# First four chunks with the masks ahead of the conversions and no zero products between; row tiles 2 to 5 converted whole

## The chip, the cores and the metric

One core of one Trainium2 chip. The time is device microseconds (us) of one launch. The engines are named as in the profile: PE (TensorE), DVE (VectorE), ACT (ScalarE), POOL (GpSimd) and SP (SyncE, which issues transfers).

## The reference

Three layers follow each other, all in float32; the two sets of MoE weights arrive as 64-bit floats.

```
state = gamma * state + k_t v_t^T;  y_t = scale * q_t state          # (4, 8, 768, 64) retention
x = y as (3072, 512)
h = x @ w_in (512 -> 2048);  g = h if h > 0 else exp(h) - 1;  x2 = g @ w_out (2048 -> 512)
out = max(x2 @ w1, x2 @ w2, x2 @ w3) (512 -> 768 each) @ moe2_w_out (768 -> 512)
```

## The kernel before

The 3072 tokens are six blocks of 512, each block four chunks of 128. A product of two float32 operands is made of three passes: each operand is split into a high part (float32r, written by ACT) and a low part (the rest, written by DVE), and high x high, high x low and low x high are added up in one accumulator.

The first MoE layer works through 16 row tiles f of `wa`; each holds 128 x 512 columns of `w_in` (used by `h1`, which makes 512 hidden values of a block) and 128 x 512 of `w_out` (used by `o1`, which adds to four accumulators). A weight arrives as two 32-bit words. Turning 512 columns (a half, number n; row tile f has the halves 2f and 2f + 1) into a high and a low part takes six operations: `cv_bits` (ACT scales the upper word), `cv_rest` (three DVE operations: shift, sign, lower word), `cv_high` (ACT) and `cv_low` (DVE).

The span begins with the retention of the first four chunks, which need no earlier state: `wide_scores` (PE), `wide_mask` (DVE), `wide_mix` (PE, then the high part on ACT), `wide_rest` (the low part on DVE). Between them stand `junk` products of a zeroed tile on PE. Behind them `h1` of block 0 starts. From chunk 4 on a `visit(c)` does the retention of one chunk: `values` (PE; two guard copies on ACT at L240), `open_chunk` of the next one (scores and state update on PE, mask on DVE at L182), `finish` (PE `past` at L219, high part on ACT at L251, low part on DVE at L254) and `ready` (POOL L207, L155 and L145; DVE L210 and L212). In the program, visits 4 to 6 alternate with row tiles 2 to 4 of block 0 (`lead`), then block 1 begins (`h1(1, 0)`).

In this part the order on PE, DVE, ACT, POOL and SP is the order in which the code is written: every engine takes its own list in turn, and an instruction that waits holds all behind it. `h1` ends in exp (L398), relu (L399), e (DVE L402), gh (ACT L405) and gl (DVE L410). In what follows e(0,f) is the L402 of row tile f in block 0.

Of the kernel before, what the change touches and what calls it, by code (L numbers as in the profile page):

```python
# [17 lines left out]
P = 128  # L18
# [24 lines left out]
def kernel(ctx: ExitStack, tc: tile.TileContext, qkv0, qkv, wa, wb, dmask, qdec, cols, out):  # L43
# [26 lines left out]
    def f32(ap):  # L70
        return ap.bitcast(F32)
# [187 lines left out]
    def wide_scores(c):  # L259
        qk = raw_t[c][0]  # L260
        sc = sc_t[c] = [ps_acc.tile([P, NPAIR, P], F32, tag="acc", name="sc") for _ in range(2)]
        for p, g, r, n in heads():
            nc.tensor.matmul(
                sc[g][:, n, :], qk[rows(g), p // 2, 2 + r, :], qk[rows(g), p // 2, r, :],
                start=n == 0, stop=n == NPAIR - 1,
            )

    def wide_mask(c):
        if not wide:
            wide[0] = wpool.tile([P, 2, 2, NPAIR, P], F32, tag="w", name="a")  # L270
        sc, a = sc_t.pop(c), wide[0][:, c % 2]
        for g in range(2):
            nc.vector.tensor_tensor(
                out=a[:, g].rearrange("t (i r) q -> t i r q", r=2), in0=sc[g].rearrange("t (i r) q -> t i r q", r=2),
                in1=dmask_of(g), op=ALU.mult,
            )
        a_t[c] = a
# [23 lines left out]
            nc.tensor.matmul(up[rows(g), n, :], kd[:, p, r, :], v[:, p, r, :], start=n == 0, stop=n == NPAIR - 1)  # L301
        nc.scalar.copy(home[c], up)

    w_t, half = {}, []

    sources = [wa[n // 2][:, n % 2 * 512:(n % 2 + 1) * 512] for n in range(2 * KFF)]

    raws = {}
    DEEP = 10

    def load_half(n):
        if n < len(sources):
            f = n // 2
            if f % 2 and f < DEEP:
                if n % 2 == 0:
                    raws[f] = wpool.tile([P, 2, 512, 2], I32, tag="w", name="raw")
                r = raws[f][:, n % 2]
            else:
                r = stage.tile([P, 512, 2], I32, tag="raw", name="raw")
            nc.sync.dma_start(out=r.rearrange("p n w -> p (n w)"), in_=sources[n].bitcast(I32))  # L320
            half.append(r)

    def load_halves(n):
        while len(half) < min(n, len(sources)):
            load_half(len(half))

    tmp, keys = {}, [("a", f) for f in range(KFF)]

    def cv_bits(n):
        if n // 2 >= len(keys):  # L330
            return
        t = tmp[n] = dpool.tile([P, 512], I32, tag="t", name="t")
        nc.scalar.activation(f32(t), f32(half[n][:, :, 1]), ACTF.Copy, scale=2.0 ** -112)

    def cv_rest(n):
        if n // 2 >= len(keys):
            return
        t = tmp[n]
        lo, hi = half[n][:, :, 0], half[n][:, :, 1]
        nc.vector.tensor_scalar(  # L340
            out=t, in0=t, scalar1=3, scalar2=0x7FFFFFFF, op0=ALU.logical_shift_left, op1=ALU.bitwise_and
        )
        nc.vector.scalar_tensor_tensor(  # L343
            out=t, in0=hi, scalar=-0x80000000, in1=t, op0=ALU.bitwise_and, op1=ALU.bitwise_or
        )
        nc.vector.scalar_tensor_tensor(
            out=t.bitcast(U32), in0=lo.bitcast(U32), scalar=29, in1=t.bitcast(U32),
            op0=ALU.logical_shift_right, op1=ALU.bitwise_or,
        )
        load_halves(n + 1 + (4 if n + 4 < 2 * DEEP else 2))  # L350

    def cv_high(n):
        key, c = keys[n // 2], n % 2
        if c == 0:
            w_t[key] = wpool.tile([P, 2, 2 * 512], F32R, tag="w", name="w")
        nc.scalar.copy(w_t[key][:, 0, c * 512:(c + 1) * 512], f32(tmp[n]))  # L356

    def cv_low(n):
        key, c = keys[n // 2], n % 2
        w = w_t[key][:, :, c * 512:(c + 1) * 512]  # L360
        nc.vector.tensor_tensor(out=w[:, 1], in0=f32(tmp.pop(n)), in1=f32(w[:, 0]), op=ALU.subtract)  # L361

    PASSES = ((1, 0), (0, 1), (0, 0))

    FRESH = ((0, 0), (0, 1), (1, 0))
# [17 lines left out]
    def h1(b, f, then=(), after=(), mid=(), soon=(), next_=()):  # L383
        x = x_t[b]
        w = w_t["a", f]
        hp = ps_h.tile([P, BLK], F32, tag="h", name="hp")
        order = [(kk, pw, px) for kk in range(KDM) for pw, px in PASSES]
        if fresh(b, f):
            order = [(kk, pw, px) for pw, px in FRESH for kk in range(KDM)]
        for k, (kk, pw, px) in enumerate(order):  # L390
            nc.tensor.matmul(  # L391
                hp, w[:, pw, kk * P:(kk + 1) * P], x[px][:, kk, :],
                start=k == 0, stop=k == len(order) - 1,
            )
        e = gpool.tile([P, BLK], F32, tag="e", name="e", bufs=3)
        gh = gpool.tile([P, BLK], F32R, tag="gh", name="gh")
        gl = gpool.tile([P, BLK], F32R, tag="gl", name="gl")
        nc.scalar.activation(e, hp, ACTF.Exp)  # L398
        nc.scalar.activation(e, e, ACTF.Relu, scale=-1.0, bias=1.0)  # L399
        for step, n in mid:  # L400
            step(n)
        nc.vector.scalar_tensor_tensor(out=e, in0=e, scalar=-1.0, in1=hp, op0=ALU.mult, op1=ALU.max)  # L402
        for step, n in soon:
            step(n)
        nc.scalar.copy(gh, e)  # L405
        for step, n in next_:
# [414 lines left out]

    FA, FB = 5, 9
    groups = [(0, 0, FA), (1, 0, FB), (0, FA, KFF), (1, FB, KFF)]
    groups += [(b, 0, KFF) for b in range(2, NB)]
    seq = [(b, f, f0, f1) for b, f0, f1 in groups for f in range(f0, f1)]
# [38 lines left out]
    def junk(k):  # L866
        o = ps_h.tile([P, BLK], F32, tag="h", name="junk")
        for i in range(k):
            nc.tensor.matmul(o, zero[:, 0:P], zero, start=i == 0, stop=i == k - 1)
# [29 lines left out]
    def lead(f):
        n = 2 * f + 1  # L900
        cv_rest(n)
        cv_high(n)
        cv_rest(n + 1)
        cv_low(n)
        h1(0, f, (), (), (), [(cv_high, n + 1)], [(cv_low, n + 1)])

    def bits(f):
        cv_bits(2 * f + 1)
        cv_bits(2 * f + 2)
# [10 lines left out]
    wide_scores(2)  # L920
    wide_mask(2)
    cv_bits(0)
    wide_mix(1)
    cv_rest(0)
    cv_high(0)
    wide_rest(1)
    wide_scores(3)
    wide_mask(3)
    wide_mix(2)
# [258 lines left out]
```

## Time and profile before

| what | us |
|---|---|
| median of 3 runs (lowest, highest) | 974.17 (973.41, 974.77) |
| the profiled execution, its span | 975.89, 974.1 |
| PE busy | 955.2 (98% of the span) |
| DVE, ACT, POOL busy | 567.8, 347.8, 104.5 |
| chain that ended last, by engine | PE 86%, DVE 6%, issue 3%, ACT 2%, DMA 2% |

Busy time counts an instruction from start to end. A wait is read as the idle time of an engine just before an instruction, with the engine and line that ended it.

### The profile page before, as it was taken

How to read it: one execution, taken by the hardware profiler on the slowest of the kernel's cores; microseconds unless marked ns; L12 is line 12 of the kernel's file. 1: busy time of each engine (PE TensorE's matmuls, PEld its weight loads, DVE VectorE, ACT ScalarE, POOL GpSimd, SP SyncE). 2: the span in 40 equal slices, each digit the busy share in tenths (PEclk: the TensorE clock that was granted, in tenths of full speed). 3: DMA queues.
4: the chain of work that ended last, by engine and by line, in shares of the span. 5: the costliest groups of instructions: out<-in, count | busy, mean ns of one | idle time of the engine just before them, and what ended most of it. 6: DMA issues, size and time to landing. Idle time of an engine off the chain costs nothing.

```text
span 974.1 us, 16007 instructions
## 1 busy us (share of the span) xinstructions
PE 955.2 (98%) x6642; PEld 778.9 (80%) x6643; DVE 567.8 (58%) x931; ACT 347.8 (36%) x630; POOL 104.5 (11%) x136
## 2 busy tenths in 40 slices
PE   7899999999999999999999999999999999999998
PEld 4677878887888888878887888878888788888886
DVE  4886777434556565655554652577734777336650
ACT  2545565333444544454445453121210213101111
POOL 3230010123111111111100000000000000000100
PEclk9999999999999999999999999999999999999999
DMA  9843164236345555545535452556525565246602
GB/s 313 247 166 121 53 208 138 31 101 174 101 146 164 164 163 172 164 164 163 163 130 180 157 188 71 173 173 198 180 97 206 176 208 167 98 130 205 200 5 87
DMA packets 65928, 149.68 MB, mean 154 GB/s; under 512 B 5120, under 2 KB 35584, under 8 KB 59712
## 3 DMA queue, kind: packets, MB, share of 16 engines
q1 hardware_dynamic: 53472, 86.78, 27.7%
q0 software_dynamic: 8784, 55.06, 18.0%
q10 hardware_dynamic: 3600, 6.82, 1.9%
q8 instruction: 52, 0.85, 0.4%
q14 instruction: 20, 0.16, 0.1%
HBM read 114.30 MB, written 34.34 MB: 153 GB/s over the span
## 4 chain that ended last, share of the span: by engine, by line
PE 86%; DVE 6%; issue 3%; ACT 2%; DMA 2%; SPq 1%; POOL 0%; ACTq 0%; POOLq 0%; DVEq 0%
PE hp L744 25%; PE acc L429 24%; PE hp L391 23%; PE acc L804 10%; DMA x<-in_qkv 2%; PE xs L230 1%; DVE t L343 1%; PE xs L219 1%; DVE e L402 1%; PE xs L168 1%; ACT gh L405 1%; PE xs L196 1%; DVE t L340 1%; DMA x<-x2d 1%; DVE w L361 1%
## 5 line engine op out<-in xcount | busy, mean ns | idle before, releaser
L744 PE MATMUL hp<-seat,w 128*128 128x512 f32 x1134 | 259.9, 390 | 3.4 <-DVE m L753 3.4
L744 PEld LDWEIGHTS hp<-seat,w 128*128 128x128 f32 x1134 | 212.1, 188 | 49.9 <-DVE m L753 6.1
L391 PE MATMUL hp<-xh,w 128*128 128x512 f32 x768 | 246.1, 392 | 1.5 <-ACT w L356 0.8
L429 PE MATMUL acc<-gh,w 128*128 128x512 f32 x768 | 203.7, 394 | 1.6 <-ACT gh L405 0.5
L391 PEld LDWEIGHTS hp<-xh,w 128*128 128x128 f32 x768 | 144.8, 189 | 32.5 <-ACT xh L289 1.1
L429 PEld LDWEIGHTS acc<-gh,w 128*128 128x128 f32 x768 | 141.6, 188 | 34.6 <-ACT gh L405 1.7
L402 DVE SCALAR_TENSOR_TENSOR e<-e,hp 128x512 f32<-128x512 f32 x96 | 65.8, 685 | 135.0 <-ACT e L399 134.6
L391 PE MATMUL hp<-xl,w 128*128 128x512 f32 x384 | 142.6, 392 | 0.0
L429 PE MATMUL acc<-gl,w 128*128 128x512 f32 x384 | 109.6, 390 | 0.0
L398 ACT ACTIVATE e<-hp 128x512 f32<-128x512 f32 x96 | 57.1, 594 | 119.2 <-PE hp L391 113.2
L804 PE MATMUL acc<-w,g 128*128 128x512 f32 x432 | 99.1, 389 | 0.0
L410 DVE TENSOR_TENSOR gl<-e,gh 128x512 fp32r<-128x512 f32 x96 | 67.3, 701 | 49.9 <-ACT gh L405 48.2
L804 PEld LDWEIGHTS acc<-w,g 128*128 128x128 f32 x432 | 81.1, 188 | 16.8
L405 ACT CAST gh<-e 128x512 fp32r<-128x512 f32 x96 | 59.7, 621 | 88.8 <-DVE e L402 88.8
L391 PEld LDWEIGHTS hp<-xl,w 128*128 128x128 f32 x384 | 72.7, 189 | 15.6 <-DVE xl L254 0.3
L429 PEld LDWEIGHTS acc<-gl,w 128*128 128x128 f32 x384 | 72.1, 188 | 15.2
L770 ACT COPY u<-hp 128x512 f32<-128x512 f32 x27 | 15.9, 589 | 143.4 <-PE hp L744 142.4
L638 POOL DMA_DIRECT2D w<-ops_d x48 | 25.6, 533 | 381.9 <-PE hp L744 311.5
L399 ACT ACTIVATE e<-e 128x512 f32<-128x512 f32 x96 | 60.8, 633 | 3.1
L145 POOL TENSOR_TENSOR x<-x,cols_sb 128x512 f32<-128x512 f32 x24 | 27.1, 1133 | 158.8 <-DMA x<-in_qkv 158.8
L761 ACT CAST g<-e 128x512 fp32r<-128x512 f32 x36 | 22.2, 623 | 51.9 <-DVE e L758 51.5
L753 DVE TENSOR_TENSOR t<-hp,t 128x512 f32<-128x512 f32 x45 | 31.0, 689 | 12.3 <-PE hp L744 12.3
(92 smaller groups left out, 810.3 us busy)
## 6 DMA issues: line engine op xcount, KB each, us to landing
w<-ops_d POOLq DMA_DIRECT2D x48, 1024.0 KB, 5.2
x<-in_qkv SPq DMA_DIRECT2D x44, 512.0 KB, 6.1
ops_d<-m SPq DMA_DIRECT2D x66, 256.0 KB, 3.2
raw<-in_wa SPq DMA_DIRECT2D x32, 512.0 KB, 4.7
raw<-in_wb SPq DMA_DIRECT2D x24, 512.0 KB, 4.6
x<-x2d SPq DMA_DIRECT2D x6, 1024.0 KB, 6.1
x2d<-o ACTq DMA_DIRECT2D x22, 256.0 KB, 2.0
out<-dmask_sb SPq DMA_DIRECT2D x12, 256.0 KB, 2.0
```

The source lines that it names most:

```text
L145: nc.gpsimd.tensor_tensor(out=kd, in0=kd, in1=cols_sb[:, 0:H].rearrange("t (p r) -> t p r", r=2).unsqueeze(3).to_broadcast([P, NPAIR, 2, D ...
L391: nc.tensor.matmul(hp, w[:, pw, kk * P:(kk + 1) * P], x[px][:, kk, :], start=k == 0, stop=k == len(order) - 1,)
L398: nc.scalar.activation(e, hp, ACTF.Exp)
L399: nc.scalar.activation(e, e, ACTF.Relu, scale=-1.0, bias=1.0)
L402: nc.vector.scalar_tensor_tensor(out=e, in0=e, scalar=-1.0, in1=hp, op0=ALU.mult, op1=ALU.max)
L405: nc.scalar.copy(gh, e)
L410: nc.vector.tensor_tensor(out=gl, in0=e, in1=f32(gh), op=ALU.subtract)
L429: nc.tensor.matmul(acc_t[b][m], w[:, p[0], 512 + m * P:512 + (m + 1) * P], g[p[1]], start=f == f0 and p == first, stop=f == f1 - 1 and p = ...
L638: nc.gpsimd.dma_start(out=ring[n % RING][:, 0:z].rearrange("p s h t -> p (s h t)"), in_=ops_d[:, 4 * k:4 * k + z].rearrange("p s h t -> p ...
L744: nc.tensor.matmul(o, w[:, pw, kk * P:(kk + 1) * P], x[px][:, kk, :], start=first and k == 0, stop=last and k == 5, skip_group_check=True,)
L753: nc.vector.tensor_tensor(out=out, in0=a, in1=c, op=ALU.add)
L804: nc.tensor.matmul(acc, g2[f][:, px, m * P:(m + 1) * P], w[:, pw, :], start=f == 0 and i == 0, stop=f == KF2 - 1 and i == 2, skip_group_ch ...
```

## The change

In the first four chunks `junk` remains nine times ahead of the first scores, and two of the groups, eight and four, are gone. The masks of chunks 0 to 2 stand ahead of the first `cv_rest`. Row tiles 2 to 5 are loaded by one transfer each (1 MB) and converted with operations of 1024 columns (`row_bits`, `row_rest`, `row_high`, `row_low`); their low part is written behind the visit. Halves 0 to 3 and those from 12 on are converted as before.

```
-    def cv_rest(n): ...  load_halves(n + 1 + (4 if n + 4 < 2 * DEEP else 2))
+    def cv_rest(n): ...  if n > 2 * FA: load_half(n + NSTAGE)
+    def load_row(f):
+        raws[f] = wpool.tile([P, 1024, 2], I32, tag="w", name="raw")
+        nc.sync.dma_start(out=raws[f].rearrange("p n w -> p (n w)"), in_=wa[f].bitcast(I32))
+    def row_bits(f):
+        x = wpool.tile([P, 2, 1024], I32, tag="w", name="t")
+        rows_t[f] = x[:, 0], x[:, 1]
+        scaled(*rows_t[f], raws[f])
+    def row_rest(f): joined(*rows_t[f], raws[f])
+    def row_high(f):
+        w = w_t["a", f] = wpool.tile([P, 2, 2 * 512], F32R, tag="w", name="w")
+        nc.scalar.copy(w[:, 0], f32(rows_t[f][0]))
+    def row_low(f):
+        w = w_t["a", f]
+        nc.vector.tensor_tensor(out=w[:, 1], in0=f32(rows_t.pop(f)[0]), in1=f32(w[:, 0]), op=ALU.subtract)
...
     load(3, "k")
+    load_row(2)
     load(4)
+    load_row(3)
+    load(5)
...
     junk(9)
-    wide_scores(0)
-    junk(8)
-    wide_mask(0)
-    wide_scores(1)
-    junk(4)
-    wide_mask(1)
-    wide_mix(0)
-    wide_rest(0)
...
+    for c in range(CB):
+        wide_scores(c)
+        wide_mask(c)
+        if c:
+            wide_mix(c - 1)
+        if c == 0:
+            cv_bits(0)
+        elif c == 2:
+            cv_rest(0)
+            cv_high(0)
+            wide_rest(0)
+            wide_rest(1)
...
-    bits(1)
-    lead(1)
+    cv_bits(3)
+    row_bits(2)
+    cv_rest(3)
+    cv_high(3)
+    row_rest(2)
+    h1(0, 1, next_=[(row_high, 2)])
+    cv_low(3)
...
     keys_of(5)
-    bits(2)
-    lead(2)
-    load(7)
-    o1(0, 1, 0, FA)
+    row_low(2)
     for f in range(2, FA):
+        row_bits(f + 1)
+        o1(0, f - 1, 0, FA, (0, 1))
+        row_rest(f + 1)
+        h1(0, f, next_=[(row_high, f + 1)])
+        o1(0, f - 1, 0, FA, (2, 3))
...
         visit(f + 2)
-        if f + 1 < FA:
-            bits(f + 1)
-            o1(0, f, 0, FA, (0, 1))
-            lead(f + 1)
-            o1(0, f, 0, FA, (2, 3))
+        row_low(f + 1)
```

DVE at the first masks, in the kernel before (a is the masked score, xl the low part of the retention's result):

```order
L273 TENSOR_TENSOR a<-sc,dmask_sb 128x512 x4
L294 TENSOR_TENSOR xl<-xo,xh 128x4x128
L273 TENSOR_TENSOR a<-sc,dmask_sb 128x512 x2
L340 TENSOR_SCALAR t<-t 128x512
L343 SCALAR_TENSOR_TENSOR t<-raw,t 128x512
L346 SCALAR_TENSOR_TENSOR t<-raw,t 128x512
L294 TENSOR_TENSOR xl<-xo,xh 128x4x128
L273 TENSOR_TENSOR a<-sc,dmask_sb 128x512 x2
L361 TENSOR_TENSOR w<-t,w 128x512
L294 TENSOR_TENSOR xl<-xo,xh 128x4x128 x2
```

DVE at the same place in the changed kernel:

```order
L273 TENSOR_TENSOR a<-sc,dmask_sb 128x512 x6
L333 TENSOR_SCALAR t<-t 128x512
L336 SCALAR_TENSOR_TENSOR t<-raw,t 128x512
L339 SCALAR_TENSOR_TENSOR t<-raw,t 128x512
L294 TENSOR_TENSOR xl<-xo,xh 128x4x128 x2
L273 TENSOR_TENSOR a<-sc,dmask_sb 128x512 x2
L294 TENSOR_TENSOR xl<-xo,xh 128x4x128
L368 TENSOR_TENSOR w<-t,w 128x512
L294 TENSOR_TENSOR xl<-xo,xh 128x4x128
```

Two low parts of chunks (xl) moved behind the masks of chunk 2 and the first conversion.

ACT in the loop of the visits, before, from one exp to the next chunk's high parts (t<-raw is `cv_bits`, w<-t `cv_high`, cols_sb<-xs the two guard copies):

```order
L333 ACTIVATE t<-raw 128x512 x2
L356 CAST w<-t 128x512
L398 ACTIVATE e<-hp 128x512
L399 ACTIVATE e<-e 128x512
L356 CAST w<-t 128x512
L405 CAST gh<-e 128x512
L240 COPY cols_sb<-xs 128x1 x2
L251 CAST xh<-xs 128x4x64 x2
```

ACT in the loop of the changed kernel (w<-t of 1024 columns is `row_high`):

```order
L329 ACTIVATE t<-raw 128x1024
L424 ACTIVATE e<-hp 128x512
L425 ACTIVATE e<-e 128x512
L431 CAST gh<-e 128x512
L382 CAST w<-t 128x1024
L240 COPY cols_sb<-xs 128x1 x2
L251 CAST xh<-xs 128x4x64 x2
```

The write of a whole high part now stands between gh and the guard copies; before, both halves' writes stood ahead of gh.

DVE in the loop of the changed kernel, from e to the next e (w<-t,w of 1024 columns is `row_low`, the three behind it `row_rest`):

```order
L428 SCALAR_TENSOR_TENSOR e<-e,hp 128x512
L436 TENSOR_TENSOR gl<-e,gh 128x512
L182 TENSOR_TENSOR a<-xs,dmask_sb 128x256 x2
L254 TENSOR_TENSOR xl<-xs,xh 128x4x64 x2
L210 TENSOR_TENSOR dmask_sb<-xs,dmask_sb 128x4x64
L212 TENSOR_TENSOR states<-xs,dmask_sb 128x256
L386 TENSOR_TENSOR w<-t,w 128x1024
L333 TENSOR_SCALAR t<-t 128x1024
L336 SCALAR_TENSOR_TENSOR t<-raw,t 128x1024
L339 SCALAR_TENSOR_TENSOR t<-raw,t 128x1024
```

Before, two halves (L340, L343, L346 twice) and one low part stood between L212 and the next e, and the second low part between e and gl.

## Rows read from the trace of the kernel before

**Rows 1.** Waits of PE: engine, line, released by, total us, times, longest

```profile
PE xs L168 <- DVE e L402: 4.1, 4, 1.8
PE xo L285 <- DVE a L273: 2.1, 1, 2.1
```

**Rows 2.** Timeline of PE, 0 to 24 us: start, us, line, operation, idle before

```profile
6.00 2.08 PE L263 MATMUL sc<-x 64*128 64x128 f32 x16 [0.79 <-DMA x<-in_qkv]
...
11.12 1.16 PE L263 MATMUL sc<-x 64*128 64x128 f32 x16
...
20.59 2.14 PE L285 MATMUL xo<-a,x 128*64 128x128 f32 x16 [2.08 <-DVE a L273]
23.42 2.07 PE L391 MATMUL hp<-xh,w 128*128 128x512 f32 x4 [0.69 <-ACT xh L289]
```

**Rows 3.** Timeline of DVE, 19 to 47 us

```profile
19.86 1.27 DVE L273 TENSOR_TENSOR a<-sc,dmask_sb 128x512 f32<-128x512 f32 x2
...
24.00 0.42 DVE L340 TENSOR_SCALAR t<-t 128x512 int32<-128x512 int32 x1
...
25.18 1.42 DVE L346 SCALAR_TENSOR_TENSOR t<-raw,t 128x512 uint32<-128x512 uint32 x1
26.52 0.41 DVE L340 TENSOR_SCALAR t<-t 128x512 int32<-128x512 int32 x1
...
28.30 0.68 DVE L361 TENSOR_TENSOR w<-t,w 128x512 fp32r<-128x512 f32 x1
29.73 0.69 DVE L402 SCALAR_TENSOR_TENSOR e<-e,hp 128x512 f32<-128x512 f32 x1 [0.74 <-ACT e L399]
...
37.16 0.68 DVE L402 SCALAR_TENSOR_TENSOR e<-e,hp 128x512 f32<-128x512 f32 x1
...
46.76 0.68 DVE L402 SCALAR_TENSOR_TENSOR e<-e,hp 128x512 f32<-128x512 f32 x1
```

**Rows 4.** Timeline of POOL, 21 to 30 us

```profile
21.14 2.50 POOL L145 TENSOR_TENSOR x<-x,cols_sb 128x512 f32<-128x512 f32 x2
24.48 1.57 POOL L145 TENSOR_TENSOR x<-x,cols_sb 128x512 f32<-128x512 f32 x1 [0.84 <-DMA x<-in_qkv]
28.39 1.50 POOL L145 TENSOR_TENSOR x<-x,cols_sb 128x512 f32<-128x512 f32 x1 [2.35 <-DMA x<-in_qkv]
```

**Rows 5.** One stretch: us; PE, PEld, DVE, ACT, POOL busy; PEclk, DMA share, GB/s

```profile
21.00:22.00 1.00, 0.86 (x10) 0.82 (x10) 1.00 (x3) 0.06 (x1) 0.98 (x2) 0.50 1.17 345
```

**Rows 6.** Groups of DVE and ACT by form: busy us, mean ns, idle before

```profile
L692 DVE TENSOR_TENSOR seat<-x,seat 128x1024 fp32r<-128x1024 f32 x15 | 17.9, 1221 | 3.3 <-ACT seat L689 3.3
L689 ACT CAST seat<-x 128x1024 fp32r<-128x1024 f32 x15 | 15.2, 1048 | 0.0
```

**Rows 7.** Timeline of DVE in the loop of the visits, 55 to 65 us

```profile
55.90 0.68 DVE L402 SCALAR_TENSOR_TENSOR e<-e,hp 128x512 f32<-128x512 f32 x1
...
57.27 0.69 DVE L410 TENSOR_TENSOR gl<-e,gh 128x512 fp32r<-128x512 f32 x1
...
58.54 0.75 DVE L254 TENSOR_TENSOR xl<-xs,xh 128x256 fp32r<-128x256 f32 x2
...
59.99 0.42 DVE L340 TENSOR_SCALAR t<-t 128x512 int32<-128x512 int32 x1
60.45 1.42 DVE L343 SCALAR_TENSOR_TENSOR t<-raw,t 128x512 int32<-128x512 int32 x1
...
64.90 0.68 DVE L402 SCALAR_TENSOR_TENSOR e<-e,hp 128x512 f32<-128x512 f32 x1
```

**Rows 8.** Timeline of ACT in the loop of the visits

```profile
56.62 0.62 ACT L405 CAST gh<-e 128x512 fp32r<-128x512 f32 x1 [0.58 <-DVE e L402]
57.14 0.21 ACT L240 COPY cols_sb<-xs 128x1 f32<-128x1 f32 x2
58.11 0.65 ACT L251 CAST xh<-xs 128x256 fp32r<-128x256 f32 x2 [0.75 <-PE xs L219]
```

**Rows 9.** Timeline of POOL in the same stretch

```profile
60.00 1.31 POOL L145 TENSOR_TENSOR x<-x,cols_sb 128x512 f32<-128x512 f32 x1
```

More of the change, by code (lines that the diff above doesn't have):

```diff
@@ L302, in wide_update, with scaled, joined @@
         nc.scalar.copy(home[c], up)
-    w_t, half = {}, []
+    w_t, half = {}, {}
     sources = [wa[n // 2][:, n % 2 * 512:(n % 2 + 1) * 512] for n in range(2 * KFF)]
     raws = {}
-    DEEP = 10
     def load_half(n):
[L312 to L325, printed above, removed]
-    tmp, keys = {}, [("a", f) for f in range(KFF)]
[L329 to L339, printed above, removed]
+        if n in half or n >= len(sources):
+            return
+        if n in (2, 3):
+            if 1 not in raws:
+                raws[1] = wpool.tile([P, 2, 512, 2], I32, tag="w", name="raw")
+            r = raws[1][:, n % 2]
+        else:
+            r = stage.tile([P, 512, 2], I32, tag="raw", name="raw")
+        nc.sync.dma_start(out=r.rearrange("p n w -> p (n w)"), in_=sources[n].bitcast(I32))
+        half[n] = r
+    def load_row(f):
+        raws[f] = wpool.tile([P, 1024, 2], I32, tag="w", name="raw")
+        nc.sync.dma_start(out=raws[f].rearrange("p n w -> p (n w)"), in_=wa[f].bitcast(I32))
+    tmp, keys = {}, [("a", f) for f in range(KFF)]
+    def scaled(t, z, raw):
+        nc.scalar.activation(f32(t), f32(raw[:, :, 1]), ACTF.Copy, scale=2.0 ** -112)
+    def joined(t, z, raw):
+        lo, hi = raw[:, :, 0], raw[:, :, 1]
         nc.vector.tensor_scalar(
@@ L349, in cv_rest, with cv_bits @@
         )
-        load_halves(n + 1 + (4 if n + 4 < 2 * DEEP else 2))
+    def cv_bits(n):
+        if n // 2 >= len(keys):
+            return
+        t = dpool.tile([P, 512], I32, tag="t", name="t")
+        z = None
+        tmp[n] = t, z
+        scaled(t, z, half[n])
+    def cv_rest(n):
+        if n // 2 >= len(keys):
+            return
+        joined(*tmp[n], half[n])
+        if n > 2 * FA:
+            load_half(n + NSTAGE)
     def cv_high(n):
@@ L355, in cv_high @@
             w_t[key] = wpool.tile([P, 2, 2 * 512], F32R, tag="w", name="w")
-        nc.scalar.copy(w_t[key][:, 0, c * 512:(c + 1) * 512], f32(tmp[n]))
+        nc.scalar.copy(w_t[key][:, 0, c * 512:(c + 1) * 512], f32(tmp[n][0]))
     def cv_low(n):
@@ L360, in cv_low, with row_rest @@
         w = w_t[key][:, :, c * 512:(c + 1) * 512]
-        nc.vector.tensor_tensor(out=w[:, 1], in0=f32(tmp.pop(n)), in1=f32(w[:, 0]), op=ALU.subtract)
+        nc.vector.tensor_tensor(out=w[:, 1], in0=f32(tmp.pop(n)[0]), in1=f32(w[:, 0]), op=ALU.subtract)
+    rows_t = {}
+    def row_bits(f):
+        x = wpool.tile([P, 2, 1024], I32, tag="w", name="t")
+        rows_t[f] = x[:, 0], x[:, 1]
+        scaled(*rows_t[f], raws[f])
+    def row_rest(f):
+        joined(*rows_t[f], raws[f])
+    def row_high(f):
[4 more added lines that the diff above has]
+        nc.vector.tensor_tensor(out=w[:, 1], in0=f32(rows_t.pop(f)[0]), in1=f32(w[:, 0]), op=ALU.subtract)
+    FA, FB = 5, 9
     PASSES = ((1, 0), (0, 1), (0, 0))
@@ L820, in o2 @@
             nc.sync.dma_start(out=out[r0:r0 + P, :], in_=o)
-    FA, FB = 5, 9
     groups = [(0, 0, FA), (1, 0, FB), (0, FA, KFF), (1, FB, KFF)]
@@ L845 @@
     load(2, "qk")
-    load_halves(1)
+    load_half(0)
     load(1, "v")
@@ L850 @@
     load(3, "v")
-    load_halves(2)
+    load_half(1)
     load(0, "k")
-    load_halves(3)
+    load_half(2)
     load(1, "k")
     load(2, "k")
-    load_halves(4)
+    load_half(3)
     load(3, "k")
+    load_row(2)
     load(4)
+    load_row(3)
+    load(5)
     new_x(0)
@@ L897, in convert @@
         cv_rest(n + 1)
[L899 to L909, printed above, removed]
-    junk(9)
-    wide_scores(0)
-    junk(8)
-    wide_mask(0)
-    wide_scores(1)
-    junk(4)
-    wide_mask(1)
-    wide_mix(0)
-    wide_rest(0)
[L920 to L929, printed above, removed]
+    junk(9)
+    for c in range(CB):
[10 more added lines that the diff above has]
+            wide_rest(1)
+    wide_rest(2)
     cv_low(0)
-    wide_rest(2)
     cv_bits(1)
@@ L938 @@
     keys_of(1)
-    lead(0)
-    load(5)
+    cv_rest(1)
+    cv_high(1)
+    cv_rest(2)
+    cv_low(1)
+    h1(0, 0, soon=[(cv_high, 2)], next_=[(cv_low, 2)])
     wide_update(0)
@@ L945 @@
     keys_of(3)
-    bits(1)
-    lead(1)
-    load(6)
+    cv_bits(3)
[5 more added lines that the diff above has]
+    cv_low(3)
     wide_update(2)
@@ L957 @@
     keys_of(5)
-    bits(2)
-    lead(2)
-    load(7)
-    o1(0, 1, 0, FA)
+    row_low(2)
     for f in range(2, FA):
-        visit(f + 2)
-        if f + 1 < FA:
-            bits(f + 1)
-            o1(0, f, 0, FA, (0, 1))
-            lead(f + 1)
-            o1(0, f, 0, FA, (2, 3))
-    n = 2 * FA + 1
+        row_bits(f + 1)
[3 more added lines that the diff above has]
+        o1(0, f - 1, 0, FA, (2, 3))
+        if f + 2 <= FA:
+            load_row(f + 2)
+        else:
+            load_half(2 * FA + 2)
+            load_half(2 * FA + 3)
+        if f + 4 < EARLY:
+            load(f + 4)
+        visit(f + 2)
+        row_low(f + 1)
+    n = 2 * FA + 2
     cv_bits(n)
```

## The prediction

> **What bounds the kernel now.** I read the page first: PE is busy 955.2 of 974.1 us, so all that can be gained is in stretches where PE stands or runs slowly. Then the waits of PE: the longest sum is scores of a visit (L168) waiting for DVE's e, 4.1 us in 4 times, then the last product of the four first chunks waiting for its mask, 2.1 us [rows 1]. Both lie in the first 70 us, which is where the change is. Behind it, from `h1(1, 0)` on, PE works almost without a break, so a shift of that point is a shift of the end. Then the timelines of that stretch, engine by engine.
>
> At the head the first scores take 2.08 us and the second, behind `junk`, 1.16: PE's clock rose between them [rows 2]. PE then stands 2.08 us for the mask of chunk 3, and a stretch right after shows a granted clock of 0.50, that is 1.2 GHz [rows 2, 5]. `h1` starts at 23.42. In the loop of the visits the distance from one e to the next is 9.14 us (46.76 to 55.90) and 9.00 us (55.90 to 64.90) [rows 3, 7]. DVE has no gap in it but the one for gh, which the second low part fills; PE waits about a microsecond in each. So DVE's list sets the pace there. The reader should follow the starts of e(0,0) to e(0,4): 29.73, 37.16, 46.76, 55.90, 64.90 [rows 3, 7].
>
> **The change, step by step, as a shift of e.**
>
> *Head.* Without `junk` the second scores follow the first at 8.1 and, at the slow rate of 2.08, end at 10.1. Mask 1 follows; on PE a product and the third scores (1.4, between 2.14 and half of it, and 1.16) end at 12.6. Mask 2 takes 1.27, to 13.9; conversion 0 costs 1.78 (26.52 to 28.30) and two low parts at most 1.3. Mask 3 so starts near 16.9 and not at 19.86 [rows 2, 3]. From mask 3 to the next conversion it was 4.14 us (to 24.00), of which the product took 2.14 at the slow clock; at full clock it would be up to 0.7 less. That conversion starts at 20.3 to 21.0, over 3 us earlier. The removed `junk` itself filled waiting time; its price could only be a clock that rises later, and scores and products now run on from 6.0 without a gap, so I count nothing beyond the 0.7 left open.
>
> *What comes next there.* Two conversions (3.56) and a low part (0.65) lead to e(0,0): 24.5 to 25.2 if nothing disturbs them. But POOL's two products of 21.14 and the one of 24.48 [rows 4] now run beside them. What that costs the trace shows: L346 at 25.18 took 1.42 beside the product of 24.48, where it else takes 0.69, so 0.73 more [rows 3, 4]. Before, the two of 21.14 fell on masks and low parts read from PSUM, which kept their length. Three meetings, 2.2 us: e(0,0) at 26.7 to 27.4, say 27.1 and not 29.73: **-2.6**. Bounds: -5.2 with no meeting, -1.7 with three whole products and the slow clock.
>
> The Trainium skill (SBUF — State Buffer, "Who interferes with whom") says that a VectorE instruction with two SBUF inputs, or in a two-port mode, and a GpSimd one that reads SBUF exclude each other for the whole instruction, whichever starts first. The 1.42 agrees. By the rule alone each meeting could cost a whole product (about 1.1 us), the sum below would rise by 1.5, and wider operations hold POOL longer; by a trace in which they did not meet, it would be the first rival.
>
> *A row in one piece.* No such conversion is in the trace. DVE's only pair of widths is 1.22 us for 1024 columns and 0.68 for 512, a ratio of 0.9 to two halves [rows 3, 6]. So a row's conversion is 3.2 (two halves: 3.56) and its low part 1.1 (two: 1.2 to 1.3). Bounds: no saving, and half of it; I take 0.9, the nearest row. Four rows save 2 us of DVE's work, but what counts is where it stands.
>
> *e(0,0) to e(0,1), 7.43 before.* A whole row (3.2) stands there now in place of a half and its low part (1.78 + 0.6): +0.8. Chunk 4 is loaded behind 1 MB of row tile 2: at 345 GB/s 3.0 us later [rows 5], so POOL's product of 28.39 [rows 4] comes near 31.4, among these conversions: +0.7. Together **+1.5** (0.8 if it falls outside). ACT's list is as long as before, and PE's `h1(0,1)` is done by then.
>
> *e(0,1) to e(0,2), 9.60 before.* The low part of half 3 now stands ahead of the query decays for which POOL waits and not in the gap for gh: +0.6. `row_low` and `row_rest`, 4.3, replace two conversions and a low part, 4.16: +0.15. **+0.75**.
>
> *The loop, twice.* The same exchange, +0.15; the collision is there before (L343 1.42 at 60.45 beside POOL's 60.00 [rows 7, 9]) and meets `row_low` or `row_rest` now, at the same 0.73. New is ACT: `row_high` stands between gh and the guard copies, for which PE's `past` waits. Before, gh began at 56.62, guard at 57.14, and the high parts, released by `past`, at 58.11 [rows 8]. A cast of 1024 columns takes 1.05 [rows 6], 0.95 of it as delay. Queued behind `past` on PE are `o1` and the next `h1`; behind the high parts DVE's xl (58.54 [rows 7], where DVE came without a gap), POOL's L207, DVE's L210. All come 0.95 later, and DVE has nothing to do meanwhile, since `row_low` is behind them. +1.1 a period, **+2.2**. Bounds: 0.3 if the delay is covered, 3.4 with another meeting of 0.6 each time.
>
> *The last visit.* The same delay once more, ahead of `values(7)` and `h1(1, 0)`: **+0.95** (0 if covered). Transfers: row tiles 2 to 5 have buffers of their own and, at the rate above, land some microseconds ahead of use: 0. Later conversions are half a row ahead, where PE has no wait for them: 0.
>
> Sum: -2.6 + 1.5 + 0.75 + 2.2 + 0.95 = **+2.8**. The profiled execution took 975.89 (span 974.1, 1.8 around it) and would take 978.7; it lies 1.7 above the median of the runs, so on 974.17 I forecast **977.0**.
>
> **The rivals.** About 0.2%, 1.95 us, is what can be told from no change.
>
> 1. *The head start stays (faster).* DVE and POOL do not meet in the head, at chunk 4 or in the loop. For it: at 59.99 a shift ran in 0.42 beside POOL's 60.00 [rows 7, 9], so who comes first decides. Against it: the two rows of 1.42. Sum: -5.2 + 0.8 + 0.75 + 2.2 + 0.95 less two meetings in the loop (1.5) = -2.0: 972.2. It decides if e(0,0) starts before 25.5.
> 2. *No change.* The guard copies behind `row_high` cost nothing, because PE or DVE are late there anyway. For it: before, PE waited for e in each period, so it has a microsecond to give. Against it: DVE had none, and its xl hang on these copies. Sum: -2.6 + 1.5 + 0.75 + 0.3 = 0: 974.1.
> 3. *The clock falls in the loop.* PE now stands about 2 us in each period of 10. For it: a stand of 2.08 us was followed by 0.50 [rows 2, 5], and four products then took 2.07, twice what full clock would make of them. Against it: waits of up to 1.8 in the loop before [rows 1] were not followed by a fall. Two dozen products, those of a period, would cost 6 us more; half of it hidden by the stand itself, +3 on top of the forecast's 2.8: 980.0.
>
> That the change does not do what it says is excluded by the order of the instructions.
>
> **How the numbers follow.** Forecast 0.55, rival 1 0.13, rival 2 0.24, rival 3 0.08. The forecast's own range is 975.2 to 979.2, from the bounds of its terms (head -3.6 to -1.7, the loop and the last visit 2.2 to 4.2 together); a fifth of it lies within 0.2%. Slower by over 0.2%: 0.55 x 0.8 + 0.08 = 0.52. Within: 0.55 x 0.2 + 0.9 of rival 2 and 0.4 of rival 1 = 0.38, of which I move 0.04 out for what I did not see. Faster: the rest, 0.14. The range, 972.4 to 979.5, leaves out half of rival 1 and of rival 3.
>
> **What would show it.** In the changed profile: e(0,0) near 27, with DVE operations of over 1.2 us at 512 columns just ahead; e(0,1) near 36, e(0,2) near 46.4; distances of about 10.1 to e(0,3) and e(0,4); ACT's guard copies a microsecond behind gh's end, and a DVE gap of about 0.9 ahead of xl. The forecast is wrong if the distances stay at 9.1, or if e(0,4) starts before 64.9.

## The result and the profile after

| | us |
|---|---|
| before, median (lowest, highest) | 974.11 (973.41, 974.77) |
| after, median of 4 runs (lowest, highest) | 979.82 (979.09, 980.91) |
| ratio, 95% interval | 1.006 [1.0042, 1.0077] |
| the profiled execution of after, its span | 980.27, 978.5 |

The change costs 5.7 us where 2.8 were forecast, and 979.82 lies 0.3 above the range. The shift of e, before to after in the two profiles, in us (e(1,0) is the first e of block 1):

```
               e(0,0)  e(0,1)  e(0,2)  e(0,3)  e(0,4)  e(1,0)
before          29.73   37.16   46.76   55.90   64.90   76.91
after           27.48   36.37   46.65   56.66   66.63   79.47
difference      -2.25   -0.79   -0.11   +0.76   +1.73   +2.56
```

Where PE waits in after, from its waits (engine, line, released by, total us, times, longest):

```profile
PE hp L417 <- ACT w L363: 3.6, 1, 3.6
...
PE hp L417 <- DVE w L386: 2.7, 2, 2.0
PE xs L168 <- DVE e L428: 2.5, 4, 1.0
...
PE xs L219 <- ACT cols_sb L240: 2.0, 4, 0.6
PE xo L285 <- DVE a L273: 1.6, 2, 1.4
```

Against [rows 1] the waits for e and for the mask are shorter. In their place stand waits for conversions (w) and one for the guard copies (cols_sb), 0.6 in each visit.

DVE in after, from the last mask to e(0,2) (start, us, line, operation; answers [rows 3]):

```profile
17.06 1.28 DVE L273 TENSOR_TENSOR a<-sc,dmask_sb 128x512 f32<-128x512 f32 x2
...
21.72 2.56 DVE L339 SCALAR_TENSOR_TENSOR t<-raw,t 128x512 uint32<-128x512 uint32 x1
24.20 1.30 DVE L333 TENSOR_SCALAR t<-t 128x512 int32<-128x512 int32 x1
...
27.48 0.68 DVE L428 SCALAR_TENSOR_TENSOR e<-e,hp 128x512 f32<-128x512 f32 x1
...
31.91 1.42 DVE L339 SCALAR_TENSOR_TENSOR t<-raw,t 128x512 uint32<-128x512 uint32 x1
...
36.37 0.68 DVE L428 SCALAR_TENSOR_TENSOR e<-e,hp 128x512 f32<-128x512 f32 x1
...
46.65 0.68 DVE L428 SCALAR_TENSOR_TENSOR e<-e,hp 128x512 f32<-128x512 f32 x1
```

and POOL beside it (answers [rows 4]):

```profile
21.68 2.05 POOL L145 TENSOR_TENSOR x<-x,cols_sb 128x512 f32<-128x512 f32 x2
24.18 1.04 POOL L145 TENSOR_TENSOR x<-x,cols_sb 128x512 f32<-128x512 f32 x1 [0.46 <-DMA x<-in_qkv]
31.22 1.57 POOL L145 TENSOR_TENSOR x<-x,cols_sb 128x512 f32<-128x512 f32 x1 [5.99 <-DMA x<-in_qkv]
```

The three DVE operations that run beside POOL's take 2.56, 1.30 and 1.42 instead of 0.69, 0.42 and 0.69: 3.5 us in all. They are the meetings (a DVE operation and a POOL product at the same time) that the prediction counted: 2.75 us with three products in the head, where 2.2 were forecast, and 0.73 at chunk 4, where 0.7 was.

ACT in the loop of the visits in after (answers [rows 8]):

```profile
47.36 0.62 ACT L431 CAST gh<-e 128x512 fp32r<-128x512 f32 x1 [1.20 <-DVE e L428]
47.88 1.04 ACT L382 CAST w<-t 128x1024 fp32r<-128x1024 f32 x1
48.83 0.21 ACT L240 COPY cols_sb<-xs 128x1 f32<-128x1 f32 x2
49.65 0.65 ACT L251 CAST xh<-xs 128x256 fp32r<-128x256 f32 x2 [0.61 <-PE xs L219]
```

and DVE there (answers [rows 7]):

```profile
50.06 0.75 DVE L254 TENSOR_TENSOR xl<-xs,xh 128x256 fp32r<-128x256 f32 x2 [0.69 <-ACT xh L251]
...
51.52 2.10 DVE L386 TENSOR_TENSOR w<-t,w 128x1024 fp32r<-128x1024 f32 x1
...
56.66 0.68 DVE L428 SCALAR_TENSOR_TENSOR e<-e,hp 128x512 f32<-128x512 f32 x1
...
60.07 0.75 DVE L254 TENSOR_TENSOR xl<-xs,xh 128x256 fp32r<-128x256 f32 x2 [0.69 <-ACT xh L251]
...
61.53 1.22 DVE L386 TENSOR_TENSOR w<-t,w 128x1024 fp32r<-128x1024 f32 x1
62.66 1.53 DVE L333 TENSOR_SCALAR t<-t 128x1024 int32<-128x1024 int32 x1
...
66.63 0.68 DVE L428 SCALAR_TENSOR_TENSOR e<-e,hp 128x512 f32<-128x512 f32 x1
```

From gh's start to the guard copies it is 1.47 us; before it was 0.52 [rows 8]. DVE, which had no gap at its xl, now waits 0.69 there, and the distance of e is 10.01 and 9.97, where 9.14 and 9.00 stood.

### The profile page after: what moved, and what is told of

Its sections match the earlier page's. It is cut to its first block, busy times and chain, and to the rows that moved or that the text cites. A ratio compares the mean times of both kernels' runs of the same rounds, so it can differ in the third digit from the quotient of the medians.

```text
span 978.5 us, 15951 instructions
## 1 busy us (share of the span) xinstructions
PE 952.2 (97%) x6631; PEld 777.4 (79%) x6631; DVE 568.2 (58%) x915; ACT 346.8 (35%) x622; POOL 104.7 (11%) x136
## 3 DMA queue, kind: packets, MB, share of 16 engines
q1 hardware_dynamic: 52896, 86.78, 27.1%
## 4 chain that ended last, share of the span: by engine, by line
PE 83%; DVE 6%; DMA 3%; ACT 3%; issue 3%; SPq 1%; ACTq 0%; POOL 0%; DVEq 0%; POOLq 0%
PE hp L770 25%; PE acc L455 22%; PE hp L417 22%; PE acc L830 10%; DMA x<-in_qkv 2%; DMA ops_d<-m 1%; DVE e L428 1%; PE xs L219 1%; PE xs L230 1%; DVE t L336 1%; PE xs L168 1%; PE xs L196 1%; ACT gh L431 1%; DVE t L333 1%; DMA x<-x2d 1%
## 5 line engine op out<-in xcount | busy, mean ns | idle before, releaser
L664 POOL DMA_DIRECT2D w<-ops_d x48 | 25.5, 531 | 382.1 <-PE hp L770 311.7
```

Source lines behind the costliest of these rows:

```text
L664: nc.gpsimd.dma_start(out=ring[n % RING][:, 0:z].rearrange("p s h t -> p (s h t)"), in_=ops_d[:, 4 * k:4 * k + z].rearrange("p s h t -> p ...
```

## The experiments

Theory A, which the expectations name: the steps from e(0,0) on cost what the prediction says (guard copies behind `row_high`, meetings of DVE and POOL), and the head start of 2.6 us came of the one execution of before that was profiled. Theory F, of the last four runs, is told there. Ratios are to executions of before that were timed beside each kernel (medians 974.0 to 974.4).

**b_again: the kernel before, once more (no edit).**

> The kernel before, unchanged, profiled a second time. Between the two profiles seen so far (975.9 and 980.3 us) the start of e in block 1's first tile moved by 2.55 us (76.91 to 79.47), and e of the last tile of the first layer by 4.09 us; the medians of the runs moved by 5.7. Theory A (the first profile of before was an execution whose clock fell in the head, 1.7 us above the median): this profile lies near 974.1 and reaches that first e of block 1 at about 75.2, with e(0,0) near 28.5 and not 29.73. Theory B (the head is the same in every execution and the rest comes later): that e stays at 76.9 and the difference of 1.7 us lies behind 300 us, in waits of ACT for stores of prepared weights.

972.9 us. The first two scores on PE in this execution (start, us, line, operation):

```profile
6.18 1.16 PE L263 MATMUL sc<-x 64*128 64x128 f32 x16 [0.97 <-DMA x<-in_qkv]
...
9.11 1.16 PE L263 MATMUL sc<-x 64*128 64x128 f32 x16
```

and DVE up to e(0,0):

```profile
25.29 1.42 DVE L346 SCALAR_TENSOR_TENSOR t<-raw,t 128x512 uint32<-128x512 uint32 x1
...
27.23 0.68 DVE L402 SCALAR_TENSOR_TENSOR e<-e,hp 128x512 f32<-128x512 f32 x1
```

The first scores ran in 1.16 us and not in 2.08 [rows 2], the second stood at 9.11 and not at 11.12, and e(0,0) came at 27.23, as early as in after. The kernel is the same; what moved is when PE began to run at its full rate. The trace's first record of a granted clock of 1.00 begins at 10.6 us in before and at 5.8 here, and the duration of the same 16 products agrees. (The view by stretches prints 1.00 ahead of these records too.) A third profile of before (before_third) had e(0,0) at 27.79:

> The kernel before, unchanged, once more. Theory A (an early rise of the clock is the usual case): the rise near 5 to 6 us after the start, e(0,0) near 27.2, 973 to 974 us. Rival (the rise near 10 of the first profile is the usual case): e(0,0) near 29.7, 975.9.

974.33 us. Two of three executions have an early e(0,0), but theory A is only half met: here the clock's record begins at 9.4 and the first scores took 2.08 again. Later, ahead of e(0,0), the granted clock was 0.50 from 20.9 to 27.7 in before and from 19.5 to 22.9 in b_again, and did not fall in before_third. So the late rise by itself does not make the 2.5 us.

**x2_head_only: the new head alone**, that is before with the new order of the first four chunks and the two groups of `junk` taken out.

> The kernel before with the changed order of the first four chunks alone (masks ahead of the conversion, no junk between), row tiles converted by halves as before. Theory of the head start: e(0,0) 2 us earlier than before and nothing gives it back, as the loop is the old one: h1(1,0) about 2 us earlier, 972.2. Theory A of the second profile (before usually has no slow clock in its head): only about 1 us is won, 973.2. Rival (the head start is lost again in meetings of DVE and POOL and for data of chunk 4): 974 or more.

974.82, ratio 1.0001 [0.9991, 1.001]; e(0,0) at 27.41. In the time, the new head is worth nothing, which is what the rival said. In this profile the granted clock also fell to 0.50 in the loop, from 45 to 49 us, and the distance from e(0,2) to e(0,3) was 10.01 (9.13 in b_again).

**x3_rows_only: the rows alone**, that is after with the old head.

> The changed kernel with the old order of the first four chunks (junk between, conversion 0 ahead of mask 2); the rows converted whole stay. Theory A: the new head is worth 0 to 0.5 us, since before reaches mask 3 as early once its clock rises early: 979.5 to 980.3, the changed kernel's time. Rival (the head start of 2.2 us is real and was only lost later): 982.

979.27, ratio 1.0053 [1.0041, 1.0066]; e(0,0) 28.50, e(1,0) 80.39. The rows carry 5.3 us of the loss. This is near theory A (979.5 to 980.3) and far from the rival's 982.

**after_again, after_third: the changed kernel, twice more (no edit).**

> The changed kernel, unchanged, profiled again. A second profile of the kernel before reached e(0,0) at 27.23 us and not 29.73, mask 3 at 17.12 and not 19.86; its granted clock rose at 5.8 us and not at 10.6. Theory A (the head start of 2.25 us that the first two profiles showed was the clock of one execution of before): this profile again has e(0,0) between 27 and 28, distances of 10.0 in the loop and e(1,0) near 79.5; the runs' median is 979 to 980, 5 to 6 us above before. Rival B (a good part lies in waits behind 300 us): e of the last tile of the first layer lies more than 1 us further behind that of b_again than e(1,0) does.

979.46, ratio 1.0051 [1.0039, 1.0064]; e(0,0) 26.89, e(1,0) 79.01, and from there 899.2 us to the end of the time.

> The changed kernel, unchanged, once more. Theory A: e(0,0) near 27.2 and e(1,0) near 79, and behind e(1,0) 899 us to the end as in the kernel before, 978.5. Rival (about a microsecond behind 300 us belongs to the change): 900.5 from e(1,0) to the end, 980.

979.75; e(0,0) 26.94, e(1,0) 79.30, and 900.4 us behind it; in the first profile of after it was 900.8, in that of before 899.0. So the rival holds in two of three executions of after, and one lacks the late microsecond.

**x1_high_behind: `row_high` behind the visit.**

```
-        h1(0, f, next_=[(row_high, f + 1)])
+        h1(0, f)
...
         visit(f + 2)
+        row_high(f + 1)
         row_low(f + 1)
```

> The changed kernel with row_high (ACT, 1024 columns, 1.04 us) moved in the loop of the visits from between gh and the guard copies to behind the visit, ahead of row_low. Theory of the guard copies: PE's wait for them (0.57 us, three times) and the wait of DVE's xl (0.69 us each) go, the distances e(0,2) to e(0,3) to e(0,4) fall from 10.0 to about 9.2, and the last visit is 0.9 shorter: about 2.5 us less than the changed kernel, 977.2. Rival (DVE or POOL is late there anyway, and row_low now waits for row_high): distances stay at 9.8 or more, 979 to 980.

977.11, ratio 1.0023 [1.0012, 1.0033]: 2.4 to 2.7 us of the 5.7 come back. ACT in it:

```profile
47.24 0.62 ACT L431 CAST gh<-e 128x512 fp32r<-128x512 f32 x1 [0.75 <-DVE e L428]
48.33 0.22 ACT L240 COPY cols_sb<-xs 128x1 f32<-128x1 f32 x2 [0.47 <-PE xs L219]
...
50.08 1.06 ACT L382 CAST w<-t 128x1024 fp32r<-128x1024 f32 x1
```

The guard copies now wait for PE and not for the cast, and the second distance of e is 9.25 (56.54 to 65.79). The first stayed at 10.02, since PE ran slowly there and DVE then waited 0.69 for its scores (us; PE, PEld, DVE, ACT, POOL busy; PEclk, DMA share, GB/s):

```profile
44.00:46.00 2.00, 2.00 (x6) 1.52 (x6) 1.97 (x2) 0.74 (x2) 0.00 (x0) 0.50 1.07 370
```

The last visit took 12.09 from e(0,4) to e(1,0), and 12.84 in after.

**x4_no_keys, x5_before_no_keys: POOL's products for chunks 1 to 7 left out**, of after and of before; part of the result is left out with them.

```
-        if c >= NCHUNK:
+        if c >= NCHUNK or 0 < c < EARLY:
```

> The changed kernel without POOL's seven products of keys and decays for chunks 1 to 7 (a part of the computation that is left out). Theory of the meetings of DVE and POOL: e(0,0) about 2 us earlier than 27.48 (two long conversions of 2.56 and 1.30 fall to 0.69 and 0.42), the step to e(0,1) 0.7 shorter, two of the loop's distances 0.9 shorter: 4 to 4.7 us less than the changed kernel, 975.3. Rival (PE or ACT is the next limit in the same places): less than 2 us, 978 or more.

974.26, ratio 1.0 [0.9989, 1.0012]: 5.2 to 5.6 us less than after. DVE ahead of e(0,0):

```profile
20.45 0.69 DVE L339 SCALAR_TENSOR_TENSOR t<-raw,t 128x512 uint32<-128x512 uint32 x1
21.06 0.42 DVE L333 TENSOR_SCALAR t<-t 128x512 int32<-128x512 int32 x1
...
23.45 0.68 DVE L428 SCALAR_TENSOR_TENSOR e<-e,hp 128x512 f32<-128x512 f32 x1
```

> The kernel before without GpSimd's products for chunks 1 to 7 (part of the computation is left out). Theory A (the meetings of DVE and GpSimd cost 4 to 5 us in the changed kernel because the new order put its conversions beside those products, and less before): e(1,0) comes 1.5 to 2.5 us earlier than in the kernel before, about 972 us. Rival (the meetings cost as much before, so they are no part of the loss): 4 to 5 us earlier, 969.5.

970.25, ratio 0.9955 [0.994, 0.997]: 4.1 us less than before, nearer to the rival than to theory A. Among the waits of PE in before and after there is none for these products, so what they cost is read as meetings: 4.1 us of them in before too, and only some 1.3 of the 5.7 are new. But e(0,0) is here at

```profile
24.94 0.68 DVE L402 SCALAR_TENSOR_TENSOR e<-e,hp 128x512 f32<-128x512 f32 x1
```

and at 23.45 in the new head: without POOL the new head gains 1.5 us (in neither profile did the clock fall ahead of e(0,0)). With POOL the meetings take most of that away where the clock rises early in both: after_again has mask 3 at 15.99 and e(0,0) at 26.89, b_again 17.12 and 27.23. They do not always: in c1, below, they are 15.42 and 25.23.

**x6_clock_held: the clock held in before** by more `junk` (11 for 9 at the start, 6 ahead of the last product).

> The kernel before with two more junk products at the start (eleven, to fill the time up to the first scores) and six in the gap ahead of the last product of the first four chunks. Theory A (executions of before differ in their head by when the clock rises and falls): e(0,0) at 27.2 in the profile whatever the execution, the median 0.8 to 1.5 us under before, 973.0, and fewer runs above 975. Rival (the head is bound by data or DVE, the spread lies behind 300 us): 974.2 with the old spread, 973 to 977.5.

975.1, ratio 1.001 [1.0001, 1.0019]: a miss, since 973.0 was expected. e(0,0) 27.98, e(1,0) 75.17; the products of `h1` that follow the fill ran at full rate (four in 1.20, not 2.07), but those at 28.17 took 2.07 again. Junk moves the slow stretch, it doesn't remove it.

**x8_pairs, x9_pairs_head: conversion in pairs, another way to use 1024 columns**, that is before with halves 3 to 10 converted as the pairs (2f + 1, 2f + 2), which `lead` needs together. Scale and the three DVE operations are 1024 columns wide, high and low parts stay 512 wide; both high parts stand ahead of gh and both low parts between e and gl, ahead of the visit.

```
+        if f:
+            pair_rest(n)
+            h1(0, f, (), (), (), [(cv_high, n), (cv_high, n + 1)], [(cv_low, n), (cv_low, n + 1)])
+            return
...
-        cv_bits(2 * f + 1)
-        cv_bits(2 * f + 2)
+        pair_bits(2 * f + 1)
```

> The kernel before with its halves 3 to 10 converted in pairs as it takes them (2f+1 with 2f+2): ACT's scaling and DVE's three operations 1024 columns wide, high and low parts by halves as before, both highs between relu and gh, both lows between e and gl. Theory (width saves, the place of the parts decides): conversion 3.15 and not 3.58, one low part more than the gap for gh holds (0.6 of the 1.2 hidden): distances of 8.5 to 8.6 and not 9.0 to 9.1, e(0,4) 1.5 to 2 us earlier, 972.4. Rival (1024 columns an operation are what makes the loop slow, by longer meetings with POOL): distances 9.3 or more, 975.

972.04, ratio 0.9982 [0.9973, 0.9991]: faster than both kernels. ACT in the loop:

```profile
45.10 1.14 ACT L385 CAST w<-t 128x512 fp32r<-128x512 f32 x2 [2.85 <-DVE t L375]
46.14 0.61 ACT L434 CAST gh<-e 128x512 fp32r<-128x512 f32 x1
46.66 0.21 ACT L240 COPY cols_sb<-xs 128x1 f32<-128x1 f32 x2
```

and DVE:

```profile
44.98 0.68 DVE L431 SCALAR_TENSOR_TENSOR e<-e,hp 128x512 f32<-128x512 f32 x1
45.75 1.29 DVE L390 TENSOR_TENSOR w<-t,w 128x512 fp32r<-128x512 f32 x2
46.96 0.68 DVE L439 TENSOR_TENSOR gl<-e,gh 128x512 fp32r<-128x512 f32 x1
...
49.68 1.26 DVE L369 TENSOR_SCALAR t<-t 128x1024 int32<-128x1024 int32 x1
...
53.38 0.68 DVE L431 SCALAR_TENSOR_TENSOR e<-e,hp 128x512 f32<-128x512 f32 x1
```

Both low parts fill the time in which DVE waits for gh, the guard copies come right behind gh, and POOL's product meets a short shift. The distance of e is 8.40. Width, pairing and the place of the parts changed together here, so this run does not say what each is worth. With the new head on top:

> The half-shifted pairs of x8_pairs with the new order of the first four chunks (masks ahead of conversions, junk 8 and 4 left out). Theory A (the new head is worth what it takes from a late rise of the clock, and so nothing in a median): as x8_pairs, 972.0 us, within 1.5. Rival (the head is worth its 2.6 us, and only the row conversion behind it uses it up): 969.5. Rival (head and pairs collide with GpSimd's products at chunk 4): 973.5.

972.26, ratio 0.9973 [0.9964, 0.9983]: the head gains nothing here either.

**The late microsecond.** In the seven profiles with the new head 899.2 to 900.8 us lie behind e(1,0) (mean 900.0), in the seven with the old one 898.4 to 899.9 (mean 898.9). The pads below are not among them. The difference arises near 270 and 368 us behind e(1,0), where ACT waits for a buffer that two stores (`ops_d<-m`) free. The issue of the first two on SP in after:

```profile
343.71 1.10 SPq L535 DMA_DIRECT2D ops_d<-m  x2
```

ACT's wait for them, and the same wait in before:

```profile
350.43 0.62 ACT L592 CAST m<-t 128x512 fp32r<-128x512 f32 x1 [2.98 <-DMA ops_d<-m]
346.58 0.62 ACT L566 CAST m<-t 128x512 fp32r<-128x512 f32 x1 [1.73 <-DMA ops_d<-m]
```

and the DMA queues of after from 345.5 to 349.5 us (packets, MB, share):

```profile
q1 hardware_dynamic: 688, 1.09, 87.4%
q8 instruction: 1, 0.02, 1.5%
```

One packet of instructions lies among the stores' packets. In before there is one too, but earlier: the stores' packets (1,024 bytes each) begin 266 us behind e(1,0) in both kernels, and the instruction packet starts at 265.1 in before, ahead of them, and at 268.4 in after, among the last of them. From the packets' own times:

```
instruction packet starts,    the two stores, issued at 264.1 and 264.8,
us behind e(1,0)              land after (us)
263.5   (x6)                  4.5, 4.3   (issued 1.3 later)
264.5 to 265.1 (old head, 6)  4.4 to 5.4, 4.3 to 5.4
267.6   (x1)                  5.8, 5.7
268.1, 268.2 (after_again, x4)  4.6, 5.7 to 5.8
268.4   (after, after_third, x9)  6.6 to 6.7, 6.6
268.9   (x2)                  5.3, 6.5
```

x6 is an exception that this does not explain: its stores were not held, and 899.9 us lie behind its e(1,0), as everything in it stood 1.3 us later already when these stores were issued. No run shows why.

Theory F: the new head has 24 PE instructions fewer (12 products and their weight loads), so PE's code is fetched at other moments. That the packet is PE's code is inferred: no view names the engine, but a pad in PE's list alone moves it. Four kernels with small products (12, or 6) where PE waits for the last mask put the count back:

```
+    def pad(k):
+        o = ps_h.tile([P, BLK], F32, tag="h", name="pad")
+        for i in range(k):
+            nc.tensor.matmul(o[:, 0:32], zero[:, 0:P], zero[:, 0:32], start=i == 0, stop=i == k - 1)
...
             wide_mix(c - 1)
+        if c == 3:
+            pad(12)
```

> The changed kernel with twelve products of 32 columns on TensorE (pad) behind the third product of the first four chunks, where TensorE waits for a mask; they give back the 24 TensorE instructions that the new head left out. Theory F (behind e(1,0) the changed kernel loses about a microsecond because its shorter program shifts the 16 KB instruction fetches: one that started 265.0 us after e(1,0) in the kernel before starts at 268.4 and holds up two stores that a buffer waits for): the fetch back at 265.0, both stores landing within 5.4 us and not 6.6, 898.9 us from e(1,0) to the end and not 900.4, a median of 978.5 to 978.8. Rival (the late microsecond is chance, or comes of the rows): 979.7 as the changed kernel, stores as there.

978.62, ratio 1.0042 [1.0029, 1.0055], as forecast. The fetch is back at 265.0 and the stores land within 5.0; the queues from 343.3 to 347.3 us (the same stretch behind e(1,0) as above) hold no instructions, as the packet came ahead of them:

```profile
q1 hardware_dynamic: 716, 1.13, 87.2%
```

and ACT waits half as long as in after:

```profile
346.46 0.62 ACT L592 CAST m<-t 128x512 fp32r<-128x512 f32 x1 [1.37 <-DMA ops_d<-m]
```

The median of c1 is no test of the fetches alone. Its profile, the fastest execution of the six (976.35), also has e(0,0) at 25.23, 1.7 us ahead of the earliest in after, with no fall of the clock ahead of 24.7; and the pad keeps PE busy in a wait.

> x2_head_only (the kernel before with the new head) with the same twelve small products. Theory F: 898.9 us behind e(1,0) and not 900.0, a median of 973.6 to 973.9. Rival: 974.8 as x2_head_only.

973.63, ratio 0.9991 [0.9982, 0.9999]: as forecast. 898.9 behind e(1,0), stores 5.3, though the fetch came at 266.6 and not at 265.0.

> x9_pairs_head (pairs of halves and the new head) with the same twelve small products. Theory F: 898.8 us behind e(1,0) and not 900.2, a median of 971.0 to 971.3. Rival (the fetches cost nothing): 972.3 as x9_pairs_head.

971.72, ratio 0.997 [0.9959, 0.9982], the lowest median of a kernel that leaves nothing out; 0.4 above the forecast. The first place is mended (stores 4.4, fetch 264.6), but at the second a fetch 364.5 behind e(1,0) still held the stores for 6.1.

> The changed kernel with six of these products, half of the instructions given back. Theory F: the fetch starts near 266.7 after e(1,0), in the middle of the two stores, and the stores land between 4.6 and 6.6 us after issue; a median between 978.6 and 979.7. Rival: 979.7.

979.44, ratio 1.005 [1.0038, 1.0061]; fetch at 267.4, stores 5.3 and 5.1, 899.3 behind e(1,0). The stores land as forecast; the median lies near the rival's 979.7 and decides nothing.

The medians fall by 0.8 to 1.2 (c1), 1.2 (c3) and 0.5 (c2), each within the interval of the kernel without the pad or at its edge. Where the packet starts and when the stores land is what shows the cause. The size, about a microsecond, rests on the time behind e(1,0), which was 899.1, 898.9, 899.1 and 899.3 with a pad, where 900.0 was the mean without; one of the seven without a pad (after_again, 899.2) was as low. The medians agree with it but hold the clock as well: x2's profile had the fall in the loop, c3's had not, and that alone was 0.9 in one distance.

## Why the prediction was wrong

The direction holds, and so do the mechanisms up to e(1,0). Two steps failed: the head was sized against an unusual execution, and the work behind e(1,0) was put at nothing. How the 5.7 came about in the first two profiles: e(1,0) moved by 2.56 (forecast 2.8), another 1.82 came behind it (forecast 0), and 1.33 is that before's profile lay 1.78 above its median and after's only 0.45. Point by point:

- **Head, -2.6: the step that failed.** Against the first profile its parts came nearly as written: mask 3 at 17.06 (forecast 16.9), meetings with three products, e(0,0) at 27.48 (27.1). What was wrong is what it was measured against. Mask 3 at 19.86 [rows 3] belongs to an execution in which the clock rose late and fell again ahead of e(0,0); in the next ones of the same kernel it stood at 17.12 and 18.51, and e(0,0) at 27.23 and 27.79. The prediction saw that the profiled execution was 1.7 us above the median and took the 1.7 off at the end, but did not ask where they lay: mostly in the head which the change rewrites (2.50 of the 2.99 us between it and b_again were there at e(0,0)). Over three profiles of each kernel e(0,0) stands at 28.25 before and at 27.10 after: -1.2, not -2.6. In the time the head is worth -0.5 (c3, with the code's length kept; its interval is -1.8 to -0.1). The bound of -1.7 was also too tight by the prediction's own numbers: 25.2 and three whole products of 1.1 give 28.5, which is -1.2.
- **e(0,0) to e(1,0): +5.4 forecast, +4.8 measured** (before 47.2, 47.3, 47.6; after 52.0, 52.1, 52.4). e(0,0) to e(0,1) gave +1.46 (1.5), to e(0,2) +0.68 (0.75), the two periods +0.87 and +0.97 (1.1 each), the last visit +0.83 (0.95).
- **Guard copies behind `row_high`**: shown by x1, which gives 2.4 to 2.7 us back, a little under three times 0.95. The rest of the rows' 5.3, about half, lies ahead of that, at e(0,1) and e(0,2), as forecast.
- **Meetings of DVE and POOL**: where and how long was right, and x4 and x5 show that the new head's gain goes into them in part (23.45 against 24.94 without POOL). That they are new was mostly wrong: the products cost before 4.1 us too. In the wide operations a meeting costs up to 0.9 (2.10 for a low part that takes 1.22 where DVE began first). The rule of the Trainium skill (SBUF — State Buffer, "Who interferes with whom"), that such a pair excludes each other for the whole instruction, agrees with the 2.10 beside POOL's 1.04 at 51.49, and with 1.53 where 0.68 stands alone. The head of before has a meeting that the prediction did not read, beside POOL's product of 17.68 (1.11 us), and POOL's products of 21.14 fell there on low parts and a wait, not on masks, which ended at 21.1:

```profile
17.92 1.42 DVE L346 SCALAR_TENSOR_TENSOR t<-raw,t 128x512 uint32<-128x512 uint32 x1
```

- **Later work, 0: the other step that failed; it is about +1.** The prediction looked there for transfers and conversions of weights alone. The profiles have 1.1 us more behind e(1,0) with the new head than with the old one, and the shift of the instruction fetches is the cause found. In the kernel with the head alone it is 899.97 - 898.94 = 1.0 by the profiles and 974.82 - 973.63 = 1.2 by the medians, which hold the clock's fall in the loop as well.
- **A row in one piece**: a conversion took 3.1 (0.68, 1.23, 1.23; forecast 3.2) and a low part 1.22 (1.1). The saving was real, its place was not the path's; x8, with as wide conversions and the low parts in DVE's gap, gains 2.

In medians: head -0.5 (c3), later work +1.2 (x2 less c3), rows +5.3 (x3), together +6.0 against 5.7 measured; the rest is within the intervals.

Rival 1 (the head start stays) and rival 2 (no change) are out: e(0,0) came behind 25.5, and the guard copies cost what was said. Rival 3 gave 980.0, which is near the result, but for another reason. From 46 to 56 us of after:

```profile
46.00:56.00 10.00, 8.59 (x153) 6.63 (x152) 8.52 (x13) 4.60 (x10) 2.88 (x3) 1.00 0.24 89
```

The granted clock is 1.00, and the period is still 10.01. The clock did not fall in the loop there. In other executions, of either kernel, it did, and cost less than the 3 of rival 3: after_third had 0.50 from 45 to 48 us and a period of 10.23 (10.02 in after_again), before_third 0.50 from 47 to 50 and 9.35 (9.13 in b_again).

Open: when PE reaches its full rate at the start differs between executions, and no run here sets it.

## What to carry to other kernels

Before a gain is read from one profiled execution, ask where that execution differs from the median, above all if the difference lies in the stretch that the change rewrites; a second profile of the unchanged kernel would have shown it. Wider operations save only if they do not stand ahead of something that others wait for: as whole rows the 1024 columns cost 5 us, half of it by a high part ahead of two small copies, and as pairs with both low parts in DVE's gap they gained 2. Taking instructions out at the start can shift later code fetches of that engine, and one may land on a store that a buffer waits for.

## What the runs showed of the hardware

- An instruction fetch is a packet of 16,384 bytes on a queue of its own (q8), took about 0.95 us in after, and shares the DMA engines with data: where it started 268.1 to 268.9 us behind e(1,0), the first store that it held landed 2.4 to 2.5 us after the fetch's start (after: 268.4, and 264.24 + 6.64 = 270.9). The Trainium skill (Runtime: NRT & Kernel Launch, "Instruction fetch mechanics") says that code is refilled in blocks of 16 KiB and that crossing a boundary is mostly hidden. The size agrees; hidden it was for PE, which was busy all of 345.5 to 349.5 us, but not for the store, which landed after 6.6 us and not after 4.4 to 5.4.
- The head of one and the same kernel varied by 2.5 us (e(0,0) of before at 27.23, 27.79 and 29.73). The trace's first record of a granted clock of 1.00 began at 5.8, 9.4 and 10.6 us in these, and the first 16 products took 1.16, 2.08 and 2.08.
- A DVE shift of 512 columns, 0.42 alone, took 1.30 beside one product of POOL, and an operation of 0.69 took 2.56 beside two, 2.70 in c1.
